# A fused attention and feed-forward block: weights and attention outputs transposed by the DMA crossbar, and a new plan of banks and order

## The chip, the cores and the metric

The kernel runs on one core of one Trainium2 chip. The metric is the device time of one execution in microseconds. The core's engines are TensorE (PE, with its weight loads listed as PEld), VectorE (DVE), ScalarE (ACT), GpSimd (POOL) and SyncE (SP), which here issues nearly all transfers.

## The reference

The input is 2048 rows of 512 values. A conditioning vector makes six vectors of 512 (`sa`, `ca`, `ga`, `sb`, `cb`, `gb`). The first half of the block is a linear attention with a learned feature map, the second a gated feed-forward network:

```python
mod = silu(c) @ w_mod                      # six vectors of 512
h = layernorm(x) * (1 + ca) + sa
q, k, v = split(h @ wqkv)                  # 32 heads of 16
pq, pk = q @ w_phi, k @ w_phi              # per head, 16 x 16
phi_q = concat(softmax(pq), softmax(-pq))  # 32 features a head
phi_k = concat(softmax(pk), softmax(-pk))
kv, z = sum_s phi_k * v, sum_s phi_k
o = (phi_q @ kv) / (phi_q . z + 1e-6)
x = x + ga * (o @ wo)
h = layernorm(x) * (1 + cb) + sb
x = x + gb * ((silu(h @ w_gate) * (h @ w_up)) @ w_down)
```

`w_gate` and `w_up` are 512 x 1376, `w_down` is 1376 x 512; data are bf16.

## The kernel before, in words

The 2048 rows are 16 tiles of 128 rows, four to a chunk. All weights are loaded once, by SP, in the order of `load` calls (L291 to L304): x chunk 0, w_k, the first third of w_mod, w_v, x chunk 1, w_q, and so on.

Three stages follow each other.

**The loop over k and v tiles.** Since `w_phi` is small and block-diagonal over heads, it is folded into w_k and w_q (`fold_phi`, L458): w_k is transposed on TensorE in 16 blocks (L466), copied out of PSUM by ACT (L469), multiplied with the block-diagonal matrix `BD` (L475) and copied to `Wk2` (L478). For each tile the rows are normalised (`first_norm`, L487: statistics on DVE at L343 and L344, `veps` at L353, a power on POOL at L357, `nmr` at L361, and the normalisation at L372 on DVE or L376 on ACT), transposed on TensorE and modulated on eviction (`modulate_T`, L388, L396, L399). Then come the k product (L528), two exponentials on ACT (L538, L539), the v product (L532) and its copy (L544), the sums S over 16 features on DVE (L548), their reciprocal R (L549), and the product phi_k on POOL (L551). `kv_tile` (L554) adds each tile into eight accumulators of 128 x 129, of which only the blocks of the same head are used. `q_front` (L570) makes the exponentials `eT` of the q side, four blocks of 512 columns to a chunk (L575, L581). `gate` (L588) makes the rows `gab`, with which POOL scales `wo` (L626) and `w_down` (L630).

**The turn.** The accumulators are masked into `KVZ` (L642, L645). From then on `prepare(k)` handles two tiles: `attend` (L665) in halves of four matmuls (L675), a chain of small steps on DVE (L690 to L695) with copies of the swapped sums (L685, L686), and the weighted result `o` (L707); `turn` (L716) adds the two signs on POOL (L736) and transposes on TensorE (L735) with a copy on ACT (L739), for the first two tiles in a sum of matmuls (L726); `project` (L741) multiplies with `wo` (L748), adds into x (L751) and normalises again; `second_T` (L757) transposes and modulates.

**The products.** For each entry of `UNITS` (L32: chunk, first tile, number of tiles) the gate and up products (L786) run in 11 column groups. ACT applies silu (L793). Half of the results go through DVE (L796), half through ACT and POOL (L800, L802). The down product (L818) and the final add (L824) close a tile, and SP stores it.

The order is made by a planner written in the kernel (`Plan`, L81). Each step is recorded with an engine, an estimated duration and the buffers that it reads and writes. `set_due` gives every step a due time from the steps behind it; `run` takes the next step for the engine that can start first, among those that can start within `SLACK` of the earliest, by due time. `slots` (L227) says how many buffers of a kind there are and `quota` (L230) how many of the six single PSUM banks (`one`) a use may hold at a time. The remaining two banks are one pair (`two_ps`, L244), which holds part of the accumulators first and then one half of a tile's attention at a time. Each engine executes its steps in the planned order and waits on semaphores.

Of the kernel before, what the change touches and what calls it, by code (L numbers as in the profile page):

```python
# [14 lines left out]
P = 128  # L15
# [8 lines left out]
H = 32  # L24
# [7 lines left out]
UNITS = [(0, 0, 2), (0, 2, 2), (1, 0, 2), (1, 2, 2), (2, 0, 4), (3, 0, 4)]  # L32
# [7 lines left out]
SLACK = 0.15  # L40
STRETCH = 1.6
WAIT = 0.8
SPINE = 1.2
PACE = 11.0


class Buf:


    def __init__(self, tag=None, make=None, at=0.0, kind=None):  # L50
# [10 lines left out]
    def free_at(self):  # L61
        t = 0.0
# [7 lines left out]
class Op:  # L70
    def __init__(self, n, alts, preds, news, at, spine):
        self.n, self.alts, self.preds, self.news, self.at, self.spine = n, alts, preds, news, at, spine
        self.succs = []
# [7 lines left out]
class Plan:  # L81
    HOP = 0.2
    OWN = {"PE": 0.0, "DVE": 0.1, "ACT": 0.1, "POOL": 0.05, "SP": 0.0, "NONE": 0.0}
# [30 lines left out]
    def set_due(self):  # L114
        spine, paced = None, {}
        for o in reversed(self.ops):
            d = 0.0
            for q in o.succs:
                d = min(d, q.due - STRETCH * q.least - WAIT)
# [29 lines left out]
    def run(self):  # L149
# [6 lines left out]
        while ready:  # L156
            cand = {}
            for o in ready:
# [8 lines left out]
                if t0 is None:  # L167
                    continue
                for alt in o.alts:
# [4 lines left out]
                    cand.setdefault(eng, []).append((t, o.due, o.n, o, alt, rooms))  # L174
# [23 lines left out]
def kernel(  # L198
# [28 lines left out]
    slots = {"one": 6, "two": 1, "xn": 8, "nmr": 4, "ln2": 6, "WT": 2, "e": 3, "S": 3, "R": 3, "phik": 4,  # L227
             "va": 4, "Ssw": 2, "A": 2, "o2": 3, "o": 2, "oT": 2, "sg": 3, "gu": 13,
             "usb": 2, "ot": 3}
    quota = {"q": 1, "turn": 1, "T": 2, "wo": 1, "down": 2, "gu": 4, "kv": 4, "fold": 3}  # L230
# [13 lines left out]
    two_ps = ps.tile([P, 2, CW], FP32, name="two_ps")  # L244
    one_ps = [ps.tile([P, CW], FP32, name=f"one_ps{i}") for i in range(slots["one"])]

    def bank(kind, shape=(P, CW), dtype=FP32):

        def make(slot):
            ap = one_ps[slot][:] if dtype == FP32 else one_ps[slot][:].bitcast(dtype)  # L250
# [7 lines left out]
    def pair():  # L258
        return Buf("two", lambda slot: two_ps)

# [4 lines left out]
    wqkv_sb = wts.tile([P, KD, 3 * D], BF16, name="wqkv_sb")  # L265
# [17 lines left out]
    def load(eng, dst, src, kb):  # L283
        eng.dma_start(dst, src)
# [7 lines left out]
    at_wk = load(nc.sync, wqkv_sb[:, :, D:2 * D], wqkv_v[:, :, D:2 * D], 512)  # L292
    at_m1 = load(nc.sync, wmod_sb[:, :, 0:2 * D], wmod_v[:, :, 0:2 * D], 1024)
    at_wv = load(nc.sync, wqkv_sb[:, :, 2 * D:3 * D], wqkv_v[:, :, 2 * D:3 * D], 512)
    at_x[1] = load(nc.sync, x_ch[1][:], x_v[1], 512)
    at_wq = load(nc.sync, wqkv_sb[:, :, 0:D], wqkv_v[:, :, 0:D], 512)
# [43 lines left out]
    def stats(mv, src, reads, writes):  # L340
# [4 lines left out]
        pl.op("DVE", r=reads, w=writes, us=0.8, fn=f)  # L345

    def rstd_of(mv_t, n, bmv, name, bufs):
        b0, b, bn = Buf(), Buf(), Buf()
        st = {}

        def f1():
            st["veps"] = lnp.tile([P, n], FP32, name=name + "_veps", bufs=bufs)
            nc.vector.tensor_scalar_add(st["veps"][:], mv_t()[:, :, 1], LN_EPS)  # L353

        def f2():
            st["rstd"] = lnp.tile([P, n], FP32, name=name + "_rstd", bufs=bufs)
            nc.gpsimd.tensor_tensor(st["rstd"][:], st["veps"][:], mhalf[:, 0:n], op=ALU.pow)  # L357

        def f3():
            st["nmr"] = lnp.tile([P, n], FP32, name=name + "_nmr", bufs=bufs)  # L360
            nc.vector.scalar_tensor_tensor(st["nmr"][:], in0=mv_t()[:, :, 0], scalar=-1.0, in1=st["rstd"][:],  # L361
                                           op0=ALU.mult, op1=ALU.mult)
        pl.op("DVE", r=bmv, w=[b0], us=0.1, fn=f1)
        pl.op("POOL", r=[b0], w=[b], us=0.4 + 0.15 * n, fn=f2)
# [523 lines left out]
```

## Time and profile before

| | |
|---|---|
| time, median of 3 runs | 248.45 us (248.22 to 249.34) |
| profiled execution | 248.46 us, of which 246.7 us are its span |
| mean granted clock of TensorE | 0.979 |
| PE busy | 215.0 us (87%) |
| DVE busy | 174.6 us (71%) |
| ACT busy | 128.3 us (52%) |
| POOL busy | 101.1 us (41%) |
| moved by DMA | 13.95 MB |

The span runs from the first to the last instruction. A busy time is a sum of durations; those of matmuls overlap one another, so a full PE is not a PE at its peak. A row of a group names the line, the engine, the operation, what it writes and reads, how often it runs, then its busy time and the mean of one in ns, then the idle time of the engine ahead of it and what ended most of that. In the chain of waits each piece is what the end of the run was waiting for at that time.

### The profile page before, as it was taken

The numbers are of one execution on the slowest core, as the hardware profiler recorded it, in microseconds if no ns is written. First come the engines' busy times: TensorE is split into PE (matmuls) and PEld (weight loads), VectorE is DVE, ScalarE is ACT, GpSimd is POOL, SyncE is SP. The second block draws the span as 40 slices with busy tenths as digits, with TensorE's granted clock in tenths as the row PEclk, the third lists the DMA queues.
The fourth block names the chain that finished last, engine by engine and source line by source line (L and its number), as shares of the span: only waits on it lengthen the run. The fifth ranks groups of instructions, "written<-read, shape, count | busy, mean of one in ns | idle before, by whom it ended". The sixth has DMA issues, their size and how long they took to land.

```text
span 246.7 us, 4221 instructions
## 1 busy us (share of the span) xinstructions
PE 215.0 (87%) x1533; PEld 131.7 (53%) x1556; DVE 174.6 (71%) x461; ACT 128.3 (52%) x280; POOL 101.1 (41%) x100
## 2 busy tenths in 40 slices
PE   0799897939985879999999996999699999699994
PEld 0754555426543437777867853884345454344441
DVE  3779999996957886677767798888744798522122
ACT  2579987564763655943534524563355442355500
POOL 1117788997794011441431443353225242013300
PEclk9999999976997999999999999999999999999999
DMA  7999930000000000001001000001000001100011
GB/s 227 383 406 387 381 103 0 3 0 0 0 4 0 0 1 3 0 0 45 1 3 43 0 4 0 0 24 43 24 0 1 1 0 45 43 0 3 0 41 44
DMA packets 9062, 13.95 MB, mean 57 GB/s; under 512 B 1009, under 2 KB 6482, under 8 KB 9042
## 3 DMA queue, kind: packets, MB, share of 16 engines
q1 hardware_dynamic: 8512, 13.67, 15.4%
q8 instruction: 12, 0.20, 0.3%
q10 hardware_dynamic: 530, 0.02, 0.1%
q14 instruction: 8, 0.07, 0.1%
HBM read 11.58 MB, written 2.10 MB: 55 GB/s over the span
## 4 chain that ended last, share of the span: by engine, by line
PE 64%; DVE 24%; ACT 3%; DMA 3%; issue 3%; POOL 1%; SPq 0%; DVEq 0%; ACTq 0%
PE one_ps L786 31%; PE one_ps L818 14%; DVE S L548 5%; PE one_ps L748 5%; PE two_ps L675 3%; DVE st L343 3%; DMA wmod_sb<-in_w_mod_dram 3%; DVE xn L372 3%; PE one_ps L528 2%; PE one_ps L575 2%; DVE R L549 2%; PE one_ps L532 2%; DVE o L707 2%; ACT hT L396 2%; DVE ln_nmr L361 1%
## 5 line engine op out<-in xcount | busy, mean ns | idle before, releaser
L786 PE MATMUL one_ps<-hT,wg_sb 128*128 128x256 bf16 (+3 forms) x264 | 46.2, 308 | 1.2 <-ACT hT L396 0.9
L786 PE MATMUL one_ps<-hT,wu_sb 128*128 128x256 bf16 (+3 forms) x260 | 45.2, 307 | 0.2
L793 ACT ACTIVATE sg<-one_ps 128x512 bf16<-128x512 f32 (+2 forms) x46 | 26.3, 577 | 28.3 <-PE one_ps L786 25.2
L802 POOL TENSOR_TENSOR gu<-usb,sg 128x512 bf16<-128x512 bf16 (+1 forms) x22 | 23.5, 1070 | 42.7 <-ACT usb L800 39.9
L818 PE MATMUL one_ps<-wd_sb,gu 128*128 128x512 bf16 (+1 forms) x171 | 40.5, 379 | 0.2
L551 POOL TENSOR_TENSOR phik<-e,R 128x1024 bf16<-128x1024 bf16 x16 | 30.7, 1931 | 13.0 <-ACT hT L396 5.5
L786 PEld LDWEIGHTS <-wg_sb 128*128 128x128 bf16 (+1 forms) x264 | 25.9, 100 | 13.9 <-issue 2.1
L786 PEld LDWEIGHTS <-wu_sb 128*128 128x128 bf16 (+1 forms) x264 | 26.0, 100 | 12.2
L736 POOL TENSOR_TENSOR o<-o 128x512 bf16<-128x512 bf16 x14 | 16.1, 1152 | 38.0 <-DVE o L707 33.6
L796 DVE TENSOR_TENSOR gu<-one_ps,sg 128x512 bf16<-128x512 f32 (+1 forms) x24 | 16.3, 685 | 20.3 <-PE one_ps L786 18.4
L357 POOL TENSOR_TENSOR ln_rstd<-ln_veps,mhalf 128x1 f32<-128x1 f32 (+2 forms) x21 | 13.4, 639 | 38.3 <-DVE ln_veps L353 33.7
L818 PEld LDWEIGHTS <-gu 128*128 128x128 bf16 (+1 forms) x176 | 16.7, 98 | 17.0
L707 DVE TENSOR_TENSOR o<-two_ps,A 128x256 bf16<-128x256 f32 x64 | 24.0, 416 | 0.8
L343 DVE BATCH_NORM_STATS2 st<-x_c 128x6 f32<-128x512 bf16 x32 | 21.7, 679 | 2.7 <-DMA x_c<-in_A_x_dram 2.4
L581 ACT ACTIVATE eT<-one_ps 128x512 bf16<-128x512 f32 x32 | 17.5, 599 | 10.3 <-PE one_ps L575 10.3
L675 PE MATMUL two_ps<-KVZ,eT 128*128 128x144 bf16 x128 | 13.7, 232 | 7.3 <-DVE o L707 6.9
L548 DVE TENSOR_REDUCE S<-e 128x64 f32<-128x1024 bf16 x16 | 19.1, 1191 | 1.3 <-ACT e L539 1.2
L388 PE MATMUL one_ps<-ident_b,xn 128*128 128x128 bf16 x128 | 11.9, 236 | 7.1 <-DVE va L544 3.9
L528 PE MATMUL one_ps<-Wk,hT 128*128 128x512 bf16 x61 | 17.2, 399 | 1.0 <-ACT hT L396 0.6
L532 PE MATMUL one_ps<-wqkv_sb,hT 128*128 128x512 bf16 x62 | 17.1, 391 | 0.3 <-DVE st L343 0.2
L675 PEld LDWEIGHTS <-eT 128*128 128x128 bf16 x128 | 10.0, 100 | 13.6 <-DVE o L707 6.0
L748 PE MATMUL one_ps<-wo_sb,oT 128*128 128x512 bf16 x58 | 15.6, 380 | 1.7 <-ACT oT L739 1.4
(89 smaller groups left out, 324.6 us busy)
## 6 DMA issues: line engine op xcount, KB each, us to landing
x_c<-in_A_x_dram SPq DMA_DIRECT2D x4, 512.0 KB, 9.1
wmod_sb<-in_w_mod_dram SPq DMA_DIRECT2D x1, 2048.0 KB, 13.9
out_dram<-ot SPq DMA_DIRECT2D x16, 128.0 KB, 1.8
wqkv_sb<-in_A_wqkv_dram SPq DMA_DIRECT2D x3, 512.0 KB, 8.6
wg_sb<-in_B_w_gate_dram SPq DMA_DIRECT2D x1, 1376.0 KB, 17.5
wu_sb<-in_B_w_up_dram SPq DMA_DIRECT2D x1, 1376.0 KB, 17.7
wd_sb<-in_B_w_down_dram SPq DMA_DIRECT2D x1, 1280.0 KB, 16.5
wmod_sb<-in_w_mod_dram SPq DMA_DIRECT2D x1, 1024.0 KB, 7.6
```

What stands on the lines that cost most here:

```text
L343: nc.vector.bn_stats(st6[:], src)
L528: nc.tensor.matmul(pk()[:], lhsT=hT[c_i][k][:, cols], rhs=Wk2[:, k, :], start=(k == 0), stop=(k == KD - 1))
L532: nc.tensor.matmul(v()[:], lhsT=hT[c_i][k][:, cols], rhs=wqkv_sb[:, k, 2 * D:3 * D], start=(k == 0), stop=(k == KD - 1))
L548: pl.op("DVE", r=[e], w=[Ss], us=1.18, fn=lambda: nc.vector.tensor_reduce(Ss()[:], e()[:], axis=AX.X, op=ALU.add))
L551: pl.op("POOL", r=[e, R], w=[bphik[i]], us=1.9, fn=lambda: nc.gpsimd.tensor_tensor(bphik[i]()[:], e()[:], R()[:].unsqueeze(3).to_broadcast ...
L675: nc.tensor.matmul(nd()[:, jj, sg * NDW:(sg + 1) * NDW], lhsT=eTs[c_i, sg, j][:, ts_], rhs=KVZ[:, sg * KD + j, :], start=True, stop=True)
L707: nc.vector.tensor_tensor(o2()[:, sg, half * HK:(half + 1) * HK, :].rearrange("p j (h d) -> p j h d", d=DH), ndv()[:, :, sg, 0:P].rearrang ...
L748: nc.tensor.matmul(a()[:], lhsT=oT()[:, j, :], rhs=wo_sb[:, j, :], start=(j == 0), stop=(j == KD - 1))
L786: nc.tensor.matmul(ps_()[0:fsz, q * n:(q + 1) * n], lhsT=wt[:, k, m * P:m * P + fsz], rhs=h2[k], start=(k == 0), stop=(k == KD - 1))
L793: pl.op("ACT", r=[g, bsilu], w=[sg], us=0.2 + 0.3 * L / CW, fn=lambda: nc.scalar.activation(sg()[0:fsz, 0:L], g()[0:fsz, 0:L], ACT.Silu))
L802: pl.op("POOL", r=[usb, sg], w=[gu], us=0.1 + 1.05 * L / CW, fn=lambda: nc.gpsimd.tensor_tensor(gu()[0:fsz, 0:L], usb()[0:fsz, 0:L], sg()[ ...
L818: nc.tensor.matmul(fp()[:], lhsT=b()[0:fsz, c0:c0 + P], rhs=wd_sb[0:fsz, m, :], start=(m == 0), stop=(m == FM - 1))
```

## The change

It has several parts.

- **Crossbar loads.** w_k and w_q arrive transposed, as four transfers of 128 columns each, in the tiles `WTk` and `WTq`. The TensorE transposes and ACT copies of `fold_phi` go. w_v has a tile of its own.
- **Crossbar transposes of o.** From the third tile on, `turn` lets SP issue a transposing transfer from `o` to `oT` in place of four TensorE transposes and an ACT copy.
- **Statistics.** The small steps behind the statistics move from DVE to POOL: ten steps for a group of up to four tiles in the first normalisation, which replace the DVE aggregate too, and four for each tile in the second.
- **Accumulators.** phi_k is laid out so that four heads with both signs fill 128 rows. The eight accumulators become 128 x 65 and fit in two banks. `KVZ` is cleared at the start and filled in quarters.
- **Banks.** Two banks hold the accumulators and two of the six single ones are given up at the turn; the four together become `four_ps`, in which `attend` does a whole tile at once. Four single banks remain for everything else.
- **Order.** The scalings of `wo` stand behind the last phi_k, those of `w_down` behind the first quarter of `KVZ`. Chunk 1 is one unit of four tiles. A step may be given its engine by where it ends first. Constants, durations and quotas of the planner change.

The core of the diff:

```diff
-UNITS = [(0, 0, 2), (0, 2, 2), (1, 0, 2), (1, 2, 2), (2, 0, 4), (3, 0, 4)]
+UNITS = [(0, 0, 2), (0, 2, 2), (1, 0, 4), (2, 0, 4), (3, 0, 4)]
...
-SLACK = 0.15
+SLACK = 0.17
...
-    quota = {"q": 1, "turn": 1, "T": 2, "wo": 1, "down": 2, "gu": 4, "kv": 4, "fold": 3}
+QUOTA = {'q': 2, 'turn': 1, 'T': 3, 'T2': 3, 'wo': 2, 'down': 4, 'gu': 3, 'kv': 4, 'fold': 1}
...
-    at_wk = load(nc.sync, wqkv_sb[:, :, D:2 * D], wqkv_v[:, :, D:2 * D], 512)
+    for j in range(KD):
+        at_wk = load(nc.sync, WTk[:, j, :], A_wqkv[:, D + j * P:D + (j + 1) * P], 128, transpose=True)
...
-        pl.op("DVE", r=bmv, w=[b0], us=0.1, fn=f1)
-        pl.op("POOL", r=[b0], w=[b], us=0.4 + 0.15 * n, fn=f2)
-        pl.op("DVE", r=[b] + list(bmv), w=[bn], us=0.1, fn=f3)
+            nc.gpsimd.tensor_scalar_add(veps[:], mv_t()[:, :, 1], LN_EPS)
+            nc.gpsimd.tensor_tensor(st["rstd"][:], veps[:], mhalf[:, 0:n], op=ALU.pow)
+            nc.gpsimd.tensor_scalar(veps[:], mv_t()[:, :, 0], -1.0, None, op0=ALU.mult)
+            nc.gpsimd.tensor_tensor(st["nmr"][:], veps[:], st["rstd"][:], op=ALU.mult)
+        pl.op("POOL", r=bmv, w=[bn], us=0.8 + 0.15 * n, fn=f)
...
-                for i in range(KD):
-                    nc.tensor.transpose(tp()[:, i, :], wqkv_sb[:, i, col0 + j * P: col0 + (j + 1) * P], ident_b[:])
-            pl.op("PE", r=[bw], w=[tp], us=0.24, fn=ft)
...
+            tt(v[0], st6[:, :, 1], st6[:, :, 4], op=ALU.subtract)
+            tt(v[1], st6[:, :, 2], st6[:, :, 5], op=ALU.add)
...
+            tt(rstd[:], v[3], mhalf[:, 0:w], op=ALU.pow)
...
+            tt(nmr[:], v[4], rstd[:], op=ALU.mult)
+        pl.op("POOL", r=bst, w=[bn], us=1.6 + 0.15 * w, fn=f)
...
-                sg, j = divmod(g, KD)
-                nc.tensor.matmul(kv_acc(g // 3)[:, (g % 3) * (P + 1):(g % 3 + 1) * (P + 1)],
+                nc.tensor.matmul(kv_acc(g // 4)[:, (g % 4) * (HG + 1):(g % 4 + 1) * (HG + 1)],
...
+    for k in range(KD):
+        pl.op("POOL", r=[bgab[0], bphik[NT - 1]], w=[bwo[k]], us=1.16, fn=lambda k=k: nc.gpsimd.tensor_tensor(
+            wo_sb[:, k, :], wo_sb[:, k, :], gab[:, 0, :], op=ALU.mult))
...
+        pl.op("POOL", r=[bgab[1]] + bKVZ[0:1], w=[bwd[m]], us=1.16, fn=lambda m=m, fsz=fsz: nc.gpsimd.tensor_tensor(
+            wd_sb[0:fsz, m, :], wd_sb[0:fsz, m, :], gab[0:fsz, 1, :], op=ALU.mult))
...
+        early_cm.__exit__(None, None, None)
+        four_ps[0] = ctx.enter_context(tc.tile_pool(name="late", bufs=1, space=PSUM)).tile([P, KD, CW], FP32, name="four_ps")
...
-    def attend(n, half):
+    def attend(n):
...
-                    nc.tensor.transpose(tp()[:, j, :], o()[:, j, :], ident_b[:])
...
+            pl.op("XBAR", r=[o], w=[oT], us=2.6, fn=lambda: nc.sync.dma_start(oT()[:], o()[:], transpose=True))
```

How the order moves is shown at three places. First SP's loads, from the second one on, before:

```order
L284 DMA wqkv_sb<-in_A_wqkv_dram 128x4x512
L284 DMA wmod_sb<-in_w_mod_dram 128x4x1024
L284 DMA wqkv_sb<-in_A_wqkv_dram 128x4x512
L284 DMA x_c_80<-in_A_x_dram 128x2048
L284 DMA wqkv_sb<-in_A_wqkv_dram 128x4x512
L284 DMA x_c_81<-in_A_x_dram 128x2048
```

and after:

```order
L300 DMA_TRANSPOSE WTk<-in_A_wqkv_dram 128x512 x4
L300 DMA wmod_sb<-in_w_mod_dram 128x4x1024
L300 DMA wv_sb<-in_A_wqkv_dram 128x4x512
L300 DMA x_c_83<-in_A_x_dram 128x2048
L300 DMA_TRANSPOSE WTq<-in_A_wqkv_dram 128x512 x4
L300 DMA x_c_84<-in_A_x_dram 128x2048
```

The three kinds of wqkv become two transposed groups of four transfers and one plain load, in the places where they were.

Second POOL, from the last phi_k products on, before (`ln_rstd` is the power of the second normalisation):

```order
L551 TENSOR_TENSOR phik_512<-e_414,R_471 128x1024
L630 TENSOR_TENSOR wd_sb<-wd_sb,gab 128x512
L551 TENSOR_TENSOR phik_396<-e_350,R_391 128x1024
L551 TENSOR_TENSOR phik_436<-e_362,R_423 128x1024
L551 TENSOR_TENSOR phik_479<-e_414,R_471 128x1024
L551 TENSOR_TENSOR phik_512<-e_350,R_391 128x1024
L630 TENSOR_TENSOR wd_sb<-wd_sb,gab 128x512 x4
L630 TENSOR_TENSOR wd_sb<-wd_sb,gab 96x512
L357 TENSOR_TENSOR ln_rstd<-ln_veps,mhalf 128x1 x2
L736 TENSOR_TENSOR o_1201<-o_1150 128x512
```

and after:

```order
L579 TENSOR_TENSOR phik_502<-e_398,R_422 128x1024
L654 TENSOR_TENSOR wo_sb<-wo_sb,gab 128x512 x4
L678 TENSOR_TENSOR wd_sb<-wd_sb,gab 128x512 x8
L382 TENSOR_SCALAR ln_veps<-ln_1078 128x1
L383 TENSOR_TENSOR ln_rstd<-ln_veps,mhalf 128x1
L384 TENSOR_SCALAR ln_veps<-ln_1078 128x1
L385 TENSOR_TENSOR ln_nmr<-ln_veps,ln_rstd 128x1
L678 TENSOR_TENSOR wd_sb<-wd_sb,gab 128x512
L382 TENSOR_SCALAR ln_veps<-ln_1109 128x1
L383 TENSOR_TENSOR ln_rstd<-ln_veps,mhalf 128x1
L384 TENSOR_SCALAR ln_veps<-ln_1109 128x1
L385 TENSOR_TENSOR ln_nmr<-ln_veps,ln_rstd 128x1
```

All scalings of `wo` and `w_down` now stand behind the last phi_k, twelve of them ahead of the first tile's second norm, and each norm has four steps.

Third DVE, one tile of attention in the turn, before (`Ssw` are the swapped sums, `A` the weights of the two signs):

```order
L685 COPY Ssw_1012<-two_ps 128x2x8
L686 COPY Ssw_1012<-two_ps 128x2x8
L690 TENSOR_TENSOR U<-two_ps,Ssw_1012 128x32
L692 TENSOR_TENSOR den<-U 128x16
L694 RECIPROCAL rden<-den 128x16
L695 TENSOR_TENSOR A_1025<-Ssw_1012,rden 128x32
L707 TENSOR_TENSOR o_1003<-two_ps,A_1025 128x256 x2
```

and after:

```order
L716 COPY Ssw_1029<-four_ps 128x4x8
L717 COPY Ssw_1029<-four_ps 128x4x8
L721 TENSOR_TENSOR U<-four_ps,Ssw_1029 128x64
L723 TENSOR_TENSOR den<-U 128x32
L725 RECIPROCAL rden<-den 128x32
L726 TENSOR_TENSOR A_1042<-Ssw_1029,rden 128x64
L734 TENSOR_TENSOR o_1052<-four_ps,A_1042 128x512 x2
```

The first group handles half a tile and runs twice for each; the second handles a whole tile.

More of the change, by code (lines that the diff above doesn't have):

```diff
@@ L82 @@
     HOP = 0.2
[L83 removed]
+    OWN = {"PE": 0.0, "DVE": 0.1, "ACT": 0.1, "POOL": 0.05, "SP": 0.0, "XBAR": 0.0, "NONE": 0.0}
     def __init__(self, slots, quota):
@@ L133, in room @@
         for i in range(self.slots[b.tag]):
+            if b.tag == "one" and not (b.kind == f"last{i - 4}" if str(b.kind)[:4] == "last" else i < 4 or b.kind in EARLY):
+                continue
             old = live[b.tag].get(i)
```

295 lines of the change are left out of this document (152 added, 143 removed).

## The prediction

> **What bounds the kernel now.** I read the page first, then the stretches, the chain of waits in order of time, and the groups by line inside two stretches. The page's forty slices show two different kernels in one span:
>
> ```profile
> span 246.7 us, 4221 instructions
> PE   0799897939985879999999996999699999699994
> DVE  3779999996957886677767798888744798522122
> GB/s 227 383 406 387 381 103 0 3 0 0 0 4 0 0 1 3 0 0 45 1 3 43 0 4 0 0 24 43 24 0 1 1 0 45 43 0 3 0 41 44
> ```
>
> From about slice 15 on PE is full with few notches; before that DVE is full and PE is not. The loads fill the first five slices at some 390 GB/s. The stretches, cut where the trace changes hands (columns: length, then busy us of PE, PEld, DVE, ACT, POOL with instruction counts, clock, DMA share, GB/s):
>
> ```profile
> 9.30:71.40 62.10, 54.11 (x442) 32.98 (x448) 55.30 (x94) 45.41 (x85) 45.56 (x31) 0.95 0.40 146
> 71.40:92.60 21.20, 15.53 (x99) 8.28 (x102) 16.73 (x62) 11.61 (x27) 6.71 (x8) 0.92 0.01 1
> 92.60:243.30 150.70, 143.25 (x972) 88.63 (x986) 97.77 (x288) 68.06 (x166) 46.89 (x50) 1.00 0.04 14
> ```
>
> The loop over 16 k/v tiles (to 71.4), a turn in which the first attention tiles are made ready for the gate and up products (21.2 us), and the products themselves (150.7 us, PE busy 143.25). Behind lie 3.4 us: the last output add starts at 243.31. The pieces of the chain that I use, each with start, length, engine, tile, line:
>
> ```profile
> 9.32 1.02 PE one_ps L434 x32
> 11.21 1.71 PE one_ps L475 x16
> 17.05 1.23 DVE S L548
> 62.03 0.86 PE one_ps L532 x4
> 111.58 0.45 PE one_ps L388 x8
> 243.31 0.69 DVE ot L824
> ```
>
> PE takes up w_mod when it has landed, at 9.32. The chain reaches DVE's first sum over a tile at 17.05, and in the loop that follows DVE is busy 55.30 of 62.10 us, more than any other engine.
>
> **The change part by part.** The span is 246.7 and the profiled execution 248.46 us, so 1.8 us lie around it; the median of the runs is 248.45, the same. 0.5% of it, 1.2 us, is about what a measurement can tell.
>
> *Start.* The 16 TensorE transposes of w_k and four ACT copies go; eight crossbar loads come. No row shows a crossbar load, so I bound it:
>
> ```profile
> 1.18 0.42 SPq L284 DMA_DIRECT2D wqkv_sb<-in_A_wqkv_dram  x1
> q1 hardware_dynamic: 8512, 13.67, 15.4%
> q10 hardware_dynamic: 530, 0.02, 0.1%
> wphi_sb<-in_A_w_phi_dram ACTq DMA_DIRECT2D x1, 16.0 KB, 6.8
> out_dram<-ot SPq DMA_DIRECT2D x16, 128.0 KB, 1.8
> ```
>
> At best the same bytes cost the same: 0, or a gain if the packets flow better, which nothing here suggests. At worst the price goes by pieces. The w_phi load is 512 rows of 32 bytes and lands after 6.8 us, 5.0 more than a 128 KB output store (1.8); w_k as 128-column slices is 2048 rows of 256 bytes, so 20 us. Between them, by the queues' shares: 15.4% of 16 x 246.7 us over 8512 packets is 71 ns for 1.6 KB, 0.1% over 530 is 7 ns for 32 bytes, so some 16 ns for 256 bytes, and 2048 of them on 16 engines take 2.1 us, 0.8 more than the 1.3 that 512 KB take at 390 GB/s. Three further issues of 0.42 us come ahead of w_mod's. I take +1.5 us for w_mod, nearest to the queue rows, since w_phi shared its time with megabytes of other loads.
>
> The Trainium skill, "DMA: Bandwidth & Descriptors", section "Latency and other measured facts", gives a transposing DMA 261 GB/s with a non-contiguous middle dimension: by that estimate 512 KB take 2.0 us, and the start would slip by less than I take. No run here shows it yet.
>
> On PE the k product now follows three v products and not one: two more blocks of 0.86, 1.7 us; the four folds (1.71) are ahead of it before and after. The first S on DVE moves from 17.05 to 20.3.
>
> *Loop.* By groups in 12.6 to 72.2 (busy, mean ns, idle before):
>
> ```profile
> L548 DVE TENSOR_REDUCE S<-e 128x64 f32<-128x1024 bf16 x16 | 19.1, 1191 | 1.3 <-ACT e L539 1.2
> L343 DVE BATCH_NORM_STATS2 st<-x_c 128x6 f32<-128x512 bf16 x12 | 8.0, 666 | 0.0
> L372 DVE TENSOR_SCALAR xn<-x_c,ln_mv,ln_rstd 128x512 bf16<-128x512 bf16 x8 | 7.3, 957 | 0.0
> L361 DVE SCALAR_TENSOR_TENSOR ln_nmr<-ln_mv,ln_rstd 128x4 f32<-128x4 f32 x3 | 3.4, 1134 | 0.0
> L399 DVE TENSOR_SCALAR hT<-one_ps,modA 128x512 bf16<-128x512 bf16 x6 | 2.9, 519 | 0.0
> L344 DVE BATCH_NORM_AGGREGATE ln_mv<-st 128x2 f32<-128x6 f32 x12 | 2.2, 182 | 0.4
> L353 DVE TENSOR_SCALAR ln_veps<-ln_mv 128x4 f32<-128x4 f32 x3 | 1.7, 567 | 0.1
> L551 POOL TENSOR_TENSOR phik<-e,R 128x1024 bf16<-128x1024 bf16 x16 | 30.7, 1931 | 13.0 <-ACT hT L396 5.5 <-DVE R L549 3.9 <-PE one_ps L558 2.4
> L630 POOL TENSOR_TENSOR wd_sb<-wd_sb,gab 128x512 bf16<-128x512 bf16 x7 | 8.1, 1171 | 0.0
> L626 POOL TENSOR_TENSOR wo_sb<-wo_sb,gab 128x512 bf16<-128x512 bf16 x4 | 4.6, 1178 | 0.0
> L357 POOL TENSOR_TENSOR ln_rstd<-ln_veps,mhalf 128x4 f32<-128x4 f32 x3 | 3.0, 1006 | 0.1
> 1.25 0.10 POOL L320 MEMSET mhalf<- 128x4 f32 x1
> 86.09 0.55 POOL L357 TENSOR_TENSOR ln_rstd<-ln_veps,mhalf 128x1 f32<-128x1 f32 x1 [9.09 <-DVE ln_veps L353]
> 69.49 1.93 POOL L551 TENSOR_TENSOR phik<-e,R 128x1024 bf16<-128x1024 bf16 x1 [0.19 <-PE one_ps L575]
> ```
>
> DVE loses the aggregates, veps and nmr (1.8 of the 2.2 behind the first S, 1.7, 3.4: 6.9 us); of its six normalisations behind that point five go to ACT (4.8); four of its statistics now run ahead of it (2.7); two more hT evictions come (1.0). Net 13.4. Before, first S to end of the last phi_k took 54.4 us (17.05 to 69.49 + 1.93 = 71.4); that pace has its gaps in it, 41.0 remain, so 61.3. POOL is next: phi_k can start at about 22.2, 16 x 1.93 are 30.9, and two of the ten-step norms fall inside. A small POOL step lies between 0.10 (a memset of 128x4) and 0.55 (a power of 128x1); I take 0.2, nearer the memset since the others are multiplies and adds, so a norm costs 1.0 + 9 x 0.2 = 2.8, at most 6. That is 58.5 without a gap, 65 by the upper bound. The scalings of wo and wd, 12.7 us, leave the loop. DVE ends later by these values: I take 61.5 for the last phi_k, 9.9 earlier, and let the range hold POOL's upper bound. The kv matmuls shrink from 129 to 65 columns, on a PE that has room here: nothing.
>
> *Turn.* POOL was idle for most of the 21.2 us; now it scales first. From the last phi_k: 4 wo and 9 wd scalings at 1.17 are 15.2, two four-step norms (0.55 + 3 x 0.2) 2.3, which stand among them, then xn on ACT, T2, hT and hops:
>
> ```profile
> L376 ACT ACTIVATE xn<-x_c,ln_nmr,ln_rstd 128x512 bf16<-128x512 bf16 x6 | 4.6, 806 | 3.0 <-DVE ln_nmr L361 3.0
> 91.64 0.92 ACT hT L396 x2
> 70.90 1.08 ACT L581 ACTIVATE eT<-one_ps 128x512 bf16<-128x512 f32 x2 [0.30 <-PE one_ps L575]
> ```
>
> 0.8 + 0.45 + 0.9 and three hops of 0.2: 20.3 in all, against 21.2. ACT has a chain as long: all 32 eT now come behind its last v copy, 28 of them at 0.54 ahead of the first sg, 15.1, with copies, xn and hT about 20.5, but it starts some 3 us earlier and ends second. First gate product at 81.9.
>
> *Products.* The 56 turn transposes leave PE, the last three q products and one attention tile are now ahead of the stretch:
>
> ```profile
> L735 PE MATMUL one_ps<-ident_b,o 128*128 128x128 bf16 x56 | 5.4, 219 | 0.0
> L575 PE MATMUL one_ps<-hT,Wq 128*128 128x512 bf16 x11 | 2.9, 378 | 0.1
> L675 PE MATMUL two_ps<-KVZ,eT 128*128 128x144 bf16 x104 | 10.8, 226 | 2.8 <-DVE o L707 2.8
> ```
>
> Durations overlap, so I go by flow: 0.45 for eight 128-column matmuls makes 3.1 for 56; 3 x 0.86 = 2.6; half a microsecond for the tile: 6.2. The single unit for chunk 1 streams the same columns; it needs four tiles ready where two were enough, which nothing hides if they are late, and the range holds that. Half as many small attention steps on DVE are worth nothing by themselves, since DVE is busy 97.77 of these 150.70 us. Remaining 144.5 if the other waits stay. The o transposes by crossbar lie between 1.8 (the output store) and 6.8 us (w_phi); I take 2.6, near the store, its equal in bytes. They cost nothing while PE has other products in the meantime, which it has for some 5 us by the number of matmuls between; beyond that each microsecond comes up to seven times, once a pair of tiles. SP issues them in one line with the stores, which wait for DVE; planned in that order, I put it at 0.
>
> Sum: 81.9 + 144.5 + 3.4 + 1.8 = 231.6 us.
>
> **Rivals.** *Crossbar loads by the piece* (slower). If the price goes by rows as w_phi's does, w_k takes 20 us and w_mod, x and w_q stand behind it in one queue: 18.7 us more than the plain load's 1.3, 17 beyond my 1.5, and for w_q's again, behind which x waits inside the loop, I take 2: 231.6 + 19 = 251. It decides for slower once the start slips by some 18 us. For it: 256-byte rows. Against: w_phi travelled among 390 GB/s of other loads. The Trainium skill, "VectorE: DVE Perf Modes", section "The three transpose paths", speaks against the change the same way: 1309 ns by DMA for 128x128 against 390 on TensorE, and TensorE where PSUM will do; by that estimate the 16 blocks in a row take 21 us. The trace has TensorE's at 0.45 for eight, cheaper than the page says, plus a copy.
>
> *Four banks instead of six.* The gate and up products share four PSUM banks with T2, wo and down. If each of 45 slices makes PE wait 0.25 us, 11 us go: 243. Against it stand the evictors, which wait for PE and not PE for them:
>
> ```profile
> ACT sg L793 <- PE one_ps L786: 25.2, 35, 1.9
> DVE gu L796 <- PE one_ps L786: 18.4, 9, 2.8
> ```
>
> *Late oT*: 7 pairs x 1 to 2.5 us, 239 to 249.
>
> *Better interlock*: the loop closes at 58, POOL's norms being short, and freed DVE time removes the attention matmuls' wait of 2.8 in the products: 231.6 - 3.5 - 2.8 = 225.3.
>
> That the change does nothing is excluded: the transposes are gone from PE's order.
>
> **How the numbers follow.** Forecast 0.58, better interlock 0.15, four banks 0.14, late oT 0.06, loads by the piece 0.07. The forecast's own range is 226 to 238: loop 58 to 65, the rest of the products' waits. The whole range, 222 to 244, leaves out loads by the piece (0.07), half of late oT (0.03) and tails of the others (0.08). Faster: 0.58 + 0.15 + 0.14 + 0.03 = 0.90; within 0.5%: 0.03 of late oT; slower 0.07.
>
> **What would show it.** Right: w_mod's matmuls at about 10.8, DVE no longer full in the loop, the last phi_k ending at 58 to 65, the first gate product near 82, and a products' stretch near 144 with PE over 95% busy. The forecast is wrong if w_mod lands after 13, if the products' stretch stays at 150, or if PE's waits there name oT or an evicting engine. The turn is wrong if ACT's eT, and not POOL's norm, ends last before the first gate product.

## The result and the profile after

| | before | after |
|---|---|---|
| time, median of 4 runs | 248.33 us (246.61 to 249.34) | 228.33 us (227.7 to 235.79) |
| ratio after/before | | 0.9193, 95% interval 0.9126 to 0.926 |
| profiled execution | 248.46 us | 228.23 us |

The change takes 8.1% off the time, 20 us. Some executions of a kernel take more than its others, up to 10 us (235.79 here, and the profiled executions of two kernels below, 245.0 and 245.4 us); the ratios leave them out.

The head of the page of after, to be read against the four rows that opened the prediction:

```profile
span 226.4 us, 3824 instructions
PE   0189699899997979999999999999999999999993
DVE  5549999799648888487878664957754968421231
GB/s 156 225 310 410 386 388 182 0 0 3 0 0 3 0 0 40 32 0 73 25 23 26 46 0 23 26 48 46 23 26 25 21 26 39 57 0 0 1 51 46
```

From slice 16 to the last but one PE has no notch left. DVE is still nearly full in the loop (slices 4 to 10). The first two slices move 156 and 225 GB/s where they moved 227 and 383, and the loads end a slice later. The stretches of after, cut where the same events stand (w_mod's first product, end of the last phi_k, first gate product, last output add; columns as before):

```profile
11.93:63.31 51.38, 47.63 (x423) 26.40 (x424) 43.33 (x65) 43.13 (x78) 38.55 (x47) 0.97 0.52 181
63.31:84.76 21.45, 17.93 (x127) 9.21 (x125) 16.50 (x42) 17.01 (x34) 19.65 (x24) 1.00 0.00 1
84.76:222.74 137.98, 136.76 (x827) 75.30 (x824) 85.64 (x183) 55.89 (x116) 55.36 (x91) 1.00 0.12 29
```

In the kernel before, the first gate product starts at 92.19 by its own record; the prediction's cut at 92.6 gives 0.4 us of the products to the turn. Set against the prediction's own steps, in us (each column adds up to its profiled or predicted time):

| stretch | before | forecast | after | after less forecast |
|---|---|---|---|---|
| start, to the first S | 17.05 | 20.3 | 21.19 | +0.9 |
| first S to the end of the last phi_k | 54.35 | 41.2 | 42.12 | +0.9 |
| turn, to the first gate product | 21.2 | 20.4 | 21.45 | +1.05 |
| products | 150.7 | 144.5 | 137.98 | -6.5 |
| tail and what lies around the span | 5.2 | 5.2 | 5.49 | +0.3 |
| sum | 248.5 | 231.6 | 228.23 | -3.4 |

**The start.** The chain of waits of after, from SP's second issue on (start, length, what):

```profile
1.18 1.21 SPq L300
...
5.03 1.26 SPq L300
...
6.34 5.59 DMA wmod_sb<-in_w_mod_dram
...
11.97 1.01 PE one_ps L455 x32
```

Four transposing loads of 128 KB hold SP for 1.21 to 1.26 us each, where the plain w_k took one issue of 0.42. So w_mod is issued at 6.34 and not at 1.65. It then travels among less traffic, and PE takes it up at 11.97, 2.65 us later than before (9.32). PE has done one of the four folds of w_k by then; the other three stand behind w_mod's products, at 13.65, 15.79 and 17.92, and the k product follows at 19.0.

**The loop.** The groups of after in 12.6 to 63.3 that answer to the rows shown of before, one of POOL's ten small steps among them:

```profile
L575 DVE TENSOR_REDUCE S<-e 128x64 f32<-128x1024 bf16 x16 | 19.2, 1198 | 1.4 <-ACT e L565 1.3
L393 DVE TENSOR_SCALAR xn<-x_c,ln_rstd,ln_nmr 128x512 bf16<-128x512 bf16 x2 | 1.6, 814 | 0.0
L579 POOL TENSOR_TENSOR phik<-e,R 128x1024 bf16<-128x1024 bf16 x16 | 30.5, 1930 | 3.8 <-PE one_ps L558 2.6 <-DVE R L577 0.5 <-ACT e L565 0.4
L514 POOL TENSOR_TENSOR ln_tmp<-ln_st 128x4 f32<-128x4 f32 x3 | 0.6, 203 | 7.6 <-DVE ln_st L504 7.6
```

Two normalisations are left on DVE, the sums cost what they did, POOL's idle time ahead of phi_k falls from 13.0 to 3.8, and a small step of the norm on 128x4 takes 0.203 us.

**The products.** What PE waited for between the first gate product and the last output add, in us, times and the longest. Before:

```profile
PE two_ps L675 <- DVE o L707: 2.8, 2, 1.7
PE one_ps L388 <- DVE xn L372: 1.8, 2, 1.3
PE one_ps L748 <- ACT oT L739: 0.9, 2, 0.7
PE one_ps L786 <- ACT hT L396: 0.9, 2, 0.4
```

After, the whole list:

```profile
PE one_ps L409 <- DVE xn L393: 0.5, 1, 0.5
PE one_ps L409 <- ACT xn L397: 0.3, 1, 0.3
PE four_ps L705 <- DVE o L734: 0.2, 1, 0.2
```

No wait names oT or an engine that empties the banks of the gate and up products. PE's busy time fell from 143.25 to 136.76, 6.5 us; its idle time from 150.70 - 143.25 = 7.45 to 137.98 - 136.76 = 1.22, 6.2 us. The stretch is shorter by the two together, 12.7. The split is good to some 0.8 us: the trace of before has 972 matmuls to 986 weight loads there, so some records are missing and part of its idle time is work. The waits listed add up to 6.4 us before and 1.0 after.

### The profile page after: what moved, and what is told of

The parts are those of the page before. It is cut to its first block, busy times and chain, and to the rows that moved or that the text cites. A ratio compares the mean times of both kernels' runs of the same rounds, so it can differ in the third digit from the quotient of the medians.

```text
span 226.4 us, 3824 instructions
## 1 busy us (share of the span) xinstructions
PE 203.6 (90%) x1380; PEld 111.5 (49%) x1380; DVE 152.1 (67%) x309; ACT 118.9 (52%) x231; POOL 120.7 (53%) x194
## 4 chain that ended last, share of the span: by engine, by line
PE 56%; DVE 16%; POOL 15%; issue 4%; ACT 3%; DMA 2%; SPq 2%; POOLq 0%; DVEq 0%
PE one_ps L807 25%; PE one_ps L842 11%; POOL phik L579 8%; DVE o L734 5%; PE one_ps L558 4%; PE one_ps L767 3%; PE four_ps L705 3%; PE one_ps L409 3%; PE one_ps L554 3%; DMA wmod_sb<-in_w_mod_dram 2%; SPq L300 2%; DVE den L723 2%; POOL wo_sb L654 2%; DVE A L726 2%; ACT e L565 2%
## 5 line engine op out<-in xcount | busy, mean ns | idle before, releaser
L807 PE MATMUL one_ps<-hT,wg_sb 128*128 128x512 bf16 (+3 forms) x220 | 45.6, 337 | 0.0
L807 PE MATMUL one_ps<-hT,wu_sb 128*128 128x512 bf16 (+3 forms) x220 | 45.5, 337 | 0.0
L579 POOL TENSOR_TENSOR phik<-e,R 128x1024 bf16<-128x1024 bf16 x16 | 30.5, 1930 | 3.8 <-PE one_ps L558 2.6
L807 PEld LDWEIGHTS <-wu_sb 128*128 128x128 bf16 (+1 forms) x220 | 21.8, 100 | 15.9
L807 PEld LDWEIGHTS <-wg_sb 128*128 128x128 bf16 (+1 forms) x220 | 21.6, 100 | 15.5 <-issue 0.3
L397 ACT ACTIVATE xn<-x_c,ln_nmr,ln_rstd 128x512 bf16<-128x512 bf16 x22 | 17.2, 818 | 15.0 <-POOL ln_nmr L385 13.7
L734 DVE TENSOR_TENSOR o<-four_ps,A 128x512 bf16<-128x512 f32 x32 | 20.5, 684 | 0.4
L554 PE MATMUL one_ps<-Wk,hT 128*128 128x512 bf16 x64 | 17.5, 395 | 1.0 <-ACT hT L417 1.0
L565 ACT ACTIVATE e<-one_ps 128x512 bf16<-128x512 f32 x32 | 17.0, 600 | 2.4 <-POOL phik L579 0.9
L558 PE MATMUL one_ps<-wv_sb,hT 128*128 128x512 bf16 x64 | 17.8, 404 | 0.0
L417 ACT ACTIVATE hT<-one_ps,modB 128x256 bf16<-128x256 bf16 x16 | 8.2, 559 | 15.1 <-PE one_ps L409 15.1
L848 DVE TENSOR_TENSOR ot<-x_c,one_ps 128x512 bf16<-128x512 bf16 x16 | 10.7, 682 | 7.8 <-PE one_ps L842 7.8
L824 ACT CAST usb<-one_ps 128x512 bf16<-128x512 f32 (+1 forms) x21 | 11.8, 564 | 7.5 <-PE one_ps L807 7.5
```

The source lines that it names most:

```text
L397: nc.scalar.activation(bxn()[:], src, ACT.Identity, bias=nmr_t()[:, q:q + 1], scale=rstd_t()[:, q:q + 1])
L554: nc.tensor.matmul(pk()[:], lhsT=hT[c_i][k][:, cols], rhs=Wk2[:, k, :], start=(k == 0), stop=(k == KD - 1))
L558: nc.tensor.matmul(v()[:], lhsT=hT[c_i][k][:, cols], rhs=wv_sb[:, k, :], start=(k == 0), stop=(k == KD - 1))
L565: nc.scalar.activation(e()[:, :, sg].rearrange("p g h f -> p g (h f)"), pk()[:].rearrange("p (g n) -> p g n", g=G), ACT.Exp, scale=(1.0, - ...
L579: pl.op("POOL", r=[e, R], w=[bphik[i]], us=1.9, fn=lambda: nc.gpsimd.tensor_tensor(bphik[i]()[:].rearrange("p g s h f -> p (g s h) f"), e( ...
L734: nc.vector.tensor_tensor(o2()[:, sg].rearrange("p j (h d) -> p j h d", d=DH), ndv()[:, :, sg, 0:P].rearrange("p j (h d) -> p j h d", d=DH ...
```

## The experiments

Times are medians, ratios are to the kernel before in the same set of runs. Since the planner orders the whole program anew for every edit, each kernel also says where its stretches lie. The questions: whether the crossbar loads pay (the headline), what took the waits out of the products, and what holds the start and the turn.

### The changed kernel again, as the others' partner

> The changed kernel once more, as the mark for the runs beside it: 228.3 us, first gate product at 84.8 us of the span, products' stretch 138 us. Both theories expect the same.

228.71 us (228.21 to 235.97), ratio 0.9211 (0.9168 to 0.9253). First w_mod product at 12.2, first S at 21.3, first gate product at 84.9. The next three kernels ran beside it.

### Plain loads of w_k and w_q, TensorE transposes in the fold

```diff
-    for j in range(KD):
-        at_wk = load(nc.sync, WTk[:, j, :], A_wqkv[:, D + j * P:D + (j + 1) * P], 128, transpose=True)
+    at_wk = load(nc.sync, wk_sb[:], wqkv_v[:, :, D:2 * D], 512)
...
+                for i in range(KD):
+                    nc.tensor.transpose(tp()[:, i, :], src[:, i, j * P:(j + 1) * P], ident_b[:])
+            pl.op("PE", r=[bw], w=[tp], us=0.24, fn=ft)
```

> The changed kernel with w_k and w_q loaded plainly and transposed on TensorE again, all else kept. Theory (the crossbar loads cost the start what they save in the loop): w_mod lands at 9.3 and not at 11.9, 2.6 us earlier; 32 transposes put 1.8 us on PE and eight copies 4.7 us on ACT, in a loop where ACT is busy 43 of 51 us, so that 2 to 3 us come back: 227 to 230 us in all. Rival (the crossbar loads are a good part of the gain): 231 to 234 us. The products' stretch stays at 138 in both.

233.38 us, ratio 0.9384 (0.9336 to 0.9433): 4.7 us slower than its partner (4.3 by the ratios). The mechanism was not the one that I looked for at the start. The chain of waits there shows the load of w_phi:

```profile
1.27 6.23 DMA wphi_sb<-in_A_w_phi_dram
7.52 0.90 DVE BD L475 x4
```

Among the plain loads w_phi lands 6.2 us after its issue, and `BD`, which the folds multiply with, is made late; w_mod's products come at 14.0, the first S at 25.0. And yet the last phi_k ends at 62.9, no later than with crossbar loads (63.3). The loss stands behind it, in the turn, and but for 0.9 us not in the products:

```profile
62.90:90.60 27.70, 23.93 (x177) 12.90 (x182) 16.42 (x45) 20.14 (x41) 19.90 (x25) 0.94 0.00 1
```

PE is busy 23.93 us there, against 17.93. With one bank for the fold (`'fold': 1`), the last fold of w_q is taken up only at 63.4, so all 16 q products (in after 55 of their 64 matmuls) and 3.4 us of products with the second part of w_mod fall into the turn. I read the crossbar's worth here as that of a prompt w_q; the quota of one bank has a part in it, as the kernels with three show.

### o transposed on TensorE, as before

```diff
-            pl.op("XBAR", r=[o], w=[oT], us=2.6, fn=lambda: nc.sync.dma_start(oT()[:], o()[:], transpose=True))
-            return
+            tp = bank("turn", [P, KD, P], BF16)
...
+            pl.op("PE", r=[o], w=[tp], us=0.23, fn=f)
```

> The changed kernel with o transposed on TensorE and copied by ACT again, from the third tile on. Theory (the crossbar takes 3.1 us of work off PE and the waits were removed by the whole-tile attention): products' stretch 138 + 3.1 = 141, in all 231.5 us. Rival (the crossbar path also removed waits, and a bank for the transposes is now missing among four): the stretch goes to 144 or more, 234 us or more.

234.76 us, ratio 0.9463 (0.9423 to 0.9504), 6.05 slower than its partner. The first gate product stays at 84.9, so the loss is all in the products, the windows and waits of which are these:

```profile
84.90:229.40 144.50, 140.06 (x868) 78.28 (x879) 86.18 (x190) 63.35 (x124) 55.41 (x91) 1.00 0.05 15
```

```profile
PE one_ps L409 <- ACT xn L397: 1.7, 2, 1.2
PE one_ps L760 <- POOL o L754: 1.1, 3, 0.4
```

Busy time rises by 3.3, near the 3.1 that I had for 56 transposes; idle time by 3.2 (4.44 against 1.22), of which the listed waits give 2.4 (3.4 against 1.0), since here too some matmul records are missing. So at least half the worth of o's crossbar path is work, and the rest is waits: PE stands in its fixed order at a transpose whose `o` POOL has not finished, and at an xn of ACT, which has the copies to make too.

### w_mod's first third ahead of the crossbar loads

```diff
+    at_m1 = load(nc.sync, wmod_sb[:, :, 0:2 * D], wmod_v[:, :, 0:2 * D], 1024)
     for j in range(KD):
         at_wk = load(nc.sync, WTk[:, j, :], A_wqkv[:, D + j * P:D + (j + 1) * P], 128, transpose=True)
-    at_m1 = load(nc.sync, wmod_sb[:, :, 0:2 * D], wmod_v[:, :, 0:2 * D], 1024)
```

> The changed kernel with the first third of w_mod loaded ahead of the transposed w_k. Theory (each crossbar load holds SP for 1.25 us, and w_mod stands behind four of them): w_mod lands at about 7.5 in place of 11.9, the first S comes 1 to 2.5 us earlier, and the whole takes 226 to 227.5 us. Rival (the folded w_k ends last anyway, or the loop is bound behind it): 228 us or more.

227.41 us (226.87 to 227.77), ratio 0.9162 (0.9124 to 0.9201): 1.3 us under its partner, every run below each of the partner's, and the best version found. In the rows of PE and DVE, the first w_mod product and the first S:

```profile
7.40 1.01 PE L455 MATMUL one_ps<-silucT,wmod_sb 128*128 128x1 bf16 x32 [5.11 <-DMA wmod_sb<-in_w_mod_dram]
20.17 1.20 DVE L575 TENSOR_REDUCE S<-e 128x64 f32<-128x1024 bf16 x1
```

w_mod is there 4.6 us earlier, S only 1.0: the folds of w_k, now loaded later and still made one at a time (10.96 to 16.6), hold the k product. The first gate product comes at 83.3, 1.5 earlier than the partner's; the products take the same 138.0. So with one bank for the fold some 1.5 us of the start were to be had by this order.

### The kernel before with crossbar loads alone

```diff
-    at_wk = load(nc.sync, wqkv_sb[:, :, D:2 * D], wqkv_v[:, :, D:2 * D], 512)
+    for j in range(KD):
+        at_wk = load(nc.sync, WTk[:, j, :], A_wqkv[:, D + j * P:D + (j + 1) * P], 128, transpose=True)
...
-                for i in range(KD):
-                    nc.tensor.transpose(tp()[:, i, :], wqkv_sb[:, i, col0 + j * P: col0 + (j + 1) * P], ident_b[:])
```

> The kernel before with the crossbar loads of w_k and w_q alone. Theory (they cost the start 2.6 us, and what they take off PE and ACT is off a loop that DVE bounds): 249.5 to 251 us. Rival (they pay by themselves): 246.5 us or less.

250.93 us against 247.99, ratio 1.0117 (1.0043 to 1.0192): 1.2% slower. w_mod's products come at 12.0, 2.7 later, as in the changed kernel; but the first S stands at 17.0 and the first gate product at 92.6, within half a microsecond of where they were. The slip is absorbed. In the profiled executions 2.3 us are lost in the products, which take

```profile
92.60:245.60 153.00, 144.32 (x970) 88.72 (x983) 98.33 (x289) 67.19 (x165) 46.73 (x50) 0.99 0.04 14
```

1.1 more busy and 1.2 more idle than before, in an order that the planner made anew. Which step of that order costs it was not isolated.

### The kernel before with o by crossbar alone

```diff
-            pl.op("PE", r=[o], w=[tp], us=0.23, fn=f)
+            pl.op("XBAR", r=[o], w=[oT], us=2.6, fn=lambda: nc.sync.dma_start(oT()[:], o()[:], transpose=True))
+            return
...
-             "va": 4, "Ssw": 2, "A": 2, "o2": 3, "o": 2, "oT": 2, "sg": 3, "gu": 13,
+             "va": 4, "Ssw": 2, "A": 2, "o2": 3, "o": 2, "oT": 3, "sg": 3, "gu": 13,
```

> The kernel before with the crossbar transposes of o alone (and three oT buffers). Theory (3.1 us of PE work go from a stretch that PE bounds; its waits for attention stay): 245 to 246 us. Rival (this path also removes the waits): 242 us or less. If the transfers come late: 248 us or more.

249.14 us (10 runs), ratio 1.0031 (0.9987 to 1.0075): no gain, and my expectation missed. The profiled execution, 247.54 us, lies 1.6 under that median. The products, and what PE waits for in them:

```profile
91.40:241.20 149.80, 141.67 (x914) 85.70 (x927) 98.35 (x283) 62.42 (x156) 46.82 (x50) 0.99 0.11 26
```

```profile
PE two_ps L675 <- ACT hT L396: 1.8, 1, 1.8
PE two_ps L675 <- DVE o L707: 1.4, 2, 1.3
PE one_ps L744 <- DMA oT<-o: 1.3, 2, 0.8
```

1.6 us of busy time go, but 8.1 us of idle time stay, on the single pair of attention banks and now on oT too. The same path for o is worth 6 us in the changed kernel and nothing here.

### Scalings free to run inside the loop

```diff
-        pl.op("POOL", r=[bgab[0], bphik[NT - 1]], w=[bwo[k]], us=1.16, fn=lambda k=k: nc.gpsimd.tensor_tensor(
+        pl.op("POOL", r=[bgab[0]], w=[bwo[k]], us=1.16, fn=lambda k=k: nc.gpsimd.tensor_tensor(
...
-        pl.op("POOL", r=[bgab[1]] + bKVZ[0:1], w=[bwd[m]], us=1.16, fn=lambda m=m, fsz=fsz: nc.gpsimd.tensor_tensor(
+        pl.op("POOL", r=[bgab[1]], w=[bwd[m]], us=1.16, fn=lambda m=m, fsz=fsz: nc.gpsimd.tensor_tensor(
```

> The changed kernel with the scalings of wo and w_down free to run within the loop again. Theory (POOL bounds the loop, so 17 us of scaling in it move its end): the last phi_k ends some 6 to 12 us later, the turn gets 3 to 4 us shorter since POOL then leaves DVE alone, in all 232 to 236 us. Rival (the loop has gaps on POOL that take the scalings up): 226 to 229 us.

227.9 us, ratio 0.9189 (0.9125 to 0.9252). No information: though allowed, the planner left every scaling behind the last phi_k, so the test did not do what it says.

### The small steps of the statistics back on DVE

```diff
-            nc.gpsimd.tensor_scalar_add(veps[:], mv_t()[:, :, 1], LN_EPS)
...
+        pl.op("DVE", r=bmv, w=[b0], us=0.1, fn=f1)
+        pl.op("POOL", r=[b0], w=[b], us=0.4 + 0.15 * n, fn=f2)
+        pl.op("DVE", r=[b] + list(bmv), w=[bn], us=0.1, fn=f3)
```

> The changed kernel with the small steps behind the statistics on DVE again, aggregates of the first norm too; the power stays on POOL. Theory (the DVE work taken out is what shortened the loop): the loop's DVE work grows by some 7 us and the last phi_k ends 3 to 7 us later, in all 231 to 235 us. Rival (POOL is the bound by now and gets lighter by 5 us of small steps): 226 to 229 us.

232.55 us, ratio 0.9365 (0.9307 to 0.9422). The first S comes at 24.1 and the last phi_k ends at 66.2, 2.9 late each: the delay arises ahead of the first S and is carried to the end. From the first S to the last phi_k the loop takes 42.2 us, as in after (42.1). The steps that return to DVE in that stretch come to 3.4 us (`veps` 1.5, `nmr` 1.0, aggregates 0.9), not 7, and DVE is busy 37.1 of it against 36.5. Its products:

```profile
87.60:226.10 138.50, 136.38 (x814) 75.61 (x825) 91.15 (x214) 50.88 (x110) 46.40 (x49) 1.00 0.13 29
```

DVE is busy 5.5 us more than in after, and the stretch is half a microsecond longer. So in this kernel the move of the small steps pays at the start, not between the first S and the last phi_k, and it is not what took the waits out of the products.

### Three banks for the fold, with crossbar and with plain loads

One word, `'fold': 1` to `'fold': 3`, in the changed kernel and in the one with plain loads:

> The changed kernel with three banks for the folding in place of one, crossbar loads kept; the partner of the next run. Theory (with one bank the four folds of w_k wait for each other's eviction, 2 us apart, so that the first k product comes late): the first S comes 1 to 2 us earlier, the two gates and w_q's fold move ahead, in all 226 to 228 us. Rival (the loop or the turn takes it up): 228 us or more.

> Plain loads and TensorE transposes of w_k and w_q with three banks for the folding. Theory (with one bank the added transposes and copies held back the folding of w_q, so that 16 q products and a fold fell into the turn; the 4.7 us were the quota's and not the load's): 1 us around the partner with crossbar loads and three banks, 226 to 229 us, turn near 21.5. Rival (the crossbar loads are worth 4 to 5 us by themselves): 231 us or more.

With crossbar loads 239.01 us (236.2 to 245.45; the four runs in the ratio have a median of 237.57), ratio 0.9576 (0.9508 to 0.9644); with plain loads 234.65 (233.17 to 236.14), ratio 0.9481 (0.9433 to 0.9529). Both missed what I expected. By ratios the plain loads are 0.0095 x 247.7 = 2.4 us better here. The intervals overlap a little (0.9508 to 0.9529), but every run with plain loads lies below every crossbar run, while with one bank they were 4.3 worse (0.0173 x 248.7). Plain loads have the first S at 16.2 now, yet the first gate product only at 88.5, 3.7 us after the changed kernel's; the time is lost again in the loop (47.8 us from the first S on) and the turn (24.6), and 3 us more in the products (140.9). So the sign of the crossbar loads hangs on the plan around them, and their worth by itself stays open.

### w_mod first and three fold banks together

The two edits above in one kernel.

> w_mod's first third ahead of the crossbar loads, and three banks for the folding. Theory (both let the loop start earlier): first S at 17 to 18.5, in all 225 to 226.5 us. Rival (the end of the loop is set by POOL and the turn by its chain, so an earlier start is waited away): 227.4 us or more, as with w_mod ahead alone.

235.28 us, ratio 0.9501 (0.9457 to 0.9546), 8 us behind w_mod first with one bank. The first S comes at 16.6, the earliest of the changed kernels with crossbar loads, and nothing is left of that. An early start alone is not what the end waits for. Where the loss lies was not isolated.

### Attention in halves through one pair of the four banks

```diff
     def attend(n):
+        for half in range(2):
+            attend_half(n, half)
...
+        js = [half * HK + jj for jj in range(HK)]
...
-            for j in range(KD):
+            for jj, j in enumerate(js):
```

> The changed kernel with attention in halves through one pair of banks again, two of the four left unused. Theory (whole-tile attention removed PE's waits for it in the products and shortened the chain in the turn): waits of 3 to 4 us for the pair return, products' stretch 141 or more, turn 1 to 2 us longer, in all 232 to 235 us. Rival (the waits went with the crossbar transposes and the freed DVE): 228 to 230 us.

257.62 us, ratio 1.0393 (1.0339 to 1.0447), slower than the kernel before. The direction held, the size was far off. Its products and their waits:

```profile
88.40:250.00 161.60, 146.47 (x832) 78.62 (x831) 96.73 (x280) 56.45 (x122) 55.91 (x91) 0.93 0.10 25
```

```profile
PE four_ps L710 <- DVE o L740: 7.9, 6, 2.7
PE one_ps L409 <- DVE xn L393: 5.0, 3, 3.7
PE one_ps L777 <- DMA oT<-o: 1.6, 1, 1.6
```

PE's idle time rises from 1.2 to 15.1 us: PE waits for DVE to empty the one pair, as it did before, and what follows is late too, oT among it. The kernel before has six single banks beside its pair and this one four, so it is not that kernel's attention put back, and the 15.1 may overstate what the halves cost. The other 9.7 us are busy time at a lower granted clock (0.93 against 1.00; 136.76 / 0.93 = 147.1). Why the clock is lower there was not tested.

## Why the prediction was right, and where it was not

The sign held, and the mechanism in the main: o's transposes left PE in the products, DVE's work in the loop shrank by nearly what was forecast, and the load path gave a little back. That the sum is only 3.4 us too high is in part luck: three steps ran late by 2.9 together, and the products were 6.5 early.

**Products (-6.5 us against the forecast).** The step that failed is "Remaining 144.5 if the other waits stay". The work that left PE was right: 6.2 forecast, 6.5 in busy time. The waits did not stay: 7.45 us of idle time became 1.22. The runs show what brings them back: attention in halves on one pair of banks 13.9 us of idle time, o on TensorE 3.2; DVE's small steps do not matter there. In the kernel before, o by crossbar alone leaves 8.1 us of idle time. I read this as a need for both: whole-tile attention, by which PE never waits for the first half to be emptied, and an oT for which neither PE nor ACT has work in the chain. That the two are enough is not shown: whole-tile attention alone was not put into the kernel before, and the single unit for chunk 1, the quotas and the planner's constants changed too and were not tested one by one. I had the wait of 2.8 us as a rival ("better interlock") and gave it 0.15; it and the three next to it went together.

**Start (+0.9).** "Three further issues of 0.42 us" was wrong by the kind of issue: a transposing one holds SP 1.21 to 1.26 us. w_mod slipped 2.65 us and not 1.5. The transfers themselves took 2.8 to 4.1 us from issue to landing each, so the rival of 20 us by the piece is out. The slip cost less than its size: with w_mod 4.6 us earlier the first S gained 1.0, and in the kernel before it was absorbed. What holds the first S is more the fold: the forecast kept the four folds together ahead of the k product, but with one bank three of them wait for each other behind w_mod. With three banks and w_mod's products still at 12.1, the k product comes at 15.9 and not 19.0, and the first S at 18.3.

**Loop (+0.9).** Small POOL steps at 0.2 us were right (0.203), and phi_k was unchanged. From the first S to the last phi_k DVE is busy 36.45 us against 49.09, 12.6 less where 13.4 were forecast, and the stretch is 12.2 shorter. DVE gave way to POOL, which idled only 3.8 us ahead of its 30.5: POOL's phi_k makes up 43.5% of the chain of waits in this stretch, before 3.6%. A part of DVE's old work was itself waiting beside phi_k: `nmr` on 128x4 took 1.09 to 1.21 us there, and 0.10 to 0.13 where POOL was idle (in the kernel with the steps back on DVE). Which of the parts taken off shortened the stretch stays open. It is not the small steps alone, since with them back on DVE the stretch is as long; normalisations on ACT, statistics made ahead and scalings gone from POOL are left, and no run took these back. DVE stays busy for 87% of the stretch (90% before), so "DVE no longer full" was hardly met. The granted clock is not it: it is 0.96 there in after and 1.00 with o on TensorE, and both take 42.1 us.

**Turn (+1.05).** It did not get shorter, and it lost what I thought it would gain. The order was as foreseen: POOL scales, then the norm, and xn on ACT, for which PE waits 1.2 us ahead of the first gate product; ACT's eT do not end last. POOL's row from the last phi_k to the end of the second norm took 18.4 us and not 17.5: each norm 1.5 and not 1.15, and 0.8 in which POOL waits for DVE's statistics. What I left out is DVE under POOL's scalings. Two tiles' small attention steps in the turn of after, and what POOL does meanwhile:

```profile
68.06 0.90 DVE L723 TENSOR_TENSOR den<-U 128x32 f32<-128x32 f32 x1
68.99 0.35 DVE L725 RECIPROCAL rden<-den 128x32 f32<-128x32 f32 x1
69.38 0.73 DVE L726 TENSOR_TENSOR A<-Ssw,rden 128x64 f32<-128x64 f32 x1
...
81.11 0.19 DVE L723 TENSOR_TENSOR den<-U 128x32 f32<-128x32 f32 x1
81.33 0.35 DVE L725 RECIPROCAL rden<-den 128x32 f32<-128x32 f32 x1
81.72 1.17 DVE L726 TENSOR_TENSOR A<-Ssw,rden 128x64 f32<-128x64 f32 x1
```

```profile
67.75 9.00 POOL L678 TENSOR_TENSOR wd_sb<-wd_sb,gab 128x512 bf16<-128x512 bf16 x8
77.54 0.24 POOL L382 TENSOR_SCALAR ln_veps<-ln 128x1 f32<-128x1 f32 x1 [0.79 <-DVE ln L371]
...
81.65 2.28 POOL L678 TENSOR_TENSOR wd_sb<-wd_sb,gab 128x512 bf16<-128x512 bf16 x2
```

`den` takes 0.90 while POOL scales and 0.19 while it does not; `A` takes 0.73 and 1.17 against 0.23 in the products; `rden` is 0.35 in both. The groups of the three tiles in the turn:

```profile
L726 DVE TENSOR_TENSOR A<-Ssw,rden 128x64 f32<-128x64 f32 x3 | 2.6, 876 | 0.1
L723 DVE TENSOR_TENSOR den<-U 128x32 f32<-128x32 f32 x3 | 1.7, 581 | 0.1
```

Against 0.23 and 0.19 for each that is 1.9 and 1.1 us of stretch, more than the 1.05 that the turn missed; POOL's wait of 0.8 for DVE is where it can show. That they are what lengthened it was not tested, since the kernel with free scalings did not move them.

**The signs and the rivals.** w_mod's products came at 12.0 where 10.8 was forecast, the last phi_k at 63.3 (58 to 65), the first gate product at 84.8 (82), and PE is busy 99% of the products. Four banks: no wait of PE for a bank of the gate and up products. Late oT: none in after; it shows up, at 1.3 and 1.6 us, only in the two kernels with attention in halves. Loads by the piece: excluded by the landing times, the last slice of w_k at 7.8 us. Better interlock came true in its wait, but not for its reason: with 5.5 us more of DVE work in the products they are half a microsecond longer, and the loop did not close at 58.

## What to carry to other kernels

Price a removed operation twice: its time on the engine that is full, and the waits at the place where that engine stands in order for what the operation feeds; for o's transposes here the two share 6.5 us, and in the kernel before, where attention kept its two halves, the waits did not go. A transposing load costs its queue more issue time than a plain one, so what everything waits for is issued ahead of it (w_mod first, 227.4 us). Where a planner orders the program, test a part inside both kernels, since the same edit gave 6 us in one and nothing in the other.

## What the runs showed of the hardware

- **Issue time of a transposing transfer.** SP is held 1.21 to 1.26 us for 128 KB of w_k from DRAM and 1.19 (median) for 128 KB of `o` from SBUF, against 0.42 to 0.72 for the plain 512 KB loads of w_k, w_v and w_q before; w_q's four, issued amid the other loads, took 1.3 to 2.3. Landing came 2.5 us after the issue for oT (median), 3.5 for w_k, 6.0 for w_q.
- **DVE beside POOL.** Small fp32 steps with both inputs in SBUF (`den`, `A`) that start while POOL multiplies 128x512 in SBUF stretch from about 0.2 to 0.66 to 1.17 us and end with POOL's instruction; `rden`, with one input, and `U`, with an input in PSUM (0.20 to 0.23), do not. One input is no safeguard: the normalisation `xn` on DVE takes 0.41 us alone and 1.22 here, beside a POOL multiply from 115.25 to 116.40:

```profile
115.34 1.22 DVE L393 TENSOR_SCALAR xn<-x_c,ln_rstd,ln_nmr 128x512 bf16<-128x512 bf16 x1 [1.40 <-POOL ln_nmr L385]
```

  The Trainium skill, "SBUF — State Buffer", section "SBUF: two separate sides", says that GpSimd and a DVE operation with two SBUF inputs (against a GpSimd operation that reads SBUF), or one in a two-port mode, share a pair of ports as an exclusive lock: whichever starts first has it for the whole instruction, and the other is blocked. The rows of `den` and `A` agree; whether `xn` runs in such a mode no run here shows. In the profiled executions of the two kernels with three fold banks and crossbar loads (245.0 and 245.4 us) one `den` was held far longer than one POOL instruction, until a row of eight to eleven scalings of about 1.12 us each had ended (71.39 to 83.72 in the first). This goes beyond what the page says, and why it was not let in between two of them stays open:

```profile
74.08 9.69 DVE L723 TENSOR_TENSOR den<-U 128x32 f32<-128x32 f32 x1
...
72.25 8.75 DVE L723 TENSOR_TENSOR den<-U 128x32 f32<-128x32 f32 x1
```

- **A small load's latency varies with the traffic.** The same 16 KB of w_phi landed 3.4 us after issue in after, where small transposing loads were issued ahead of w_mod. Where w_k was loaded plainly or w_mod came first it took 4.8 to 6.8 (6.8 before, 6.2 with plain loads, 6.5 with w_mod first, and 4.8 in the kernel before with o by crossbar, whose loads are those of before).
